# Moving the units that keep layer two's divided sums: out of layer one's output steps and some of layer two's token steps, into layer one's last token steps and its late mixing

## The chip, the cores and the metric

The kernel runs on one core of a Trainium2 chip. The metric is device microseconds of one execution; lower is better. A core has TensorE (PE: matmuls; its weight loads are listed apart as PEld), VectorE (DVE), ScalarE (ACT), GpSimd (POOL) and SyncE (SP). Each engine runs its own instructions in the order in which the program issues them, and waits on semaphores for what others make. SP does no arithmetic here: it issues DMA transfers, in order, and each issue can wait for the work that makes its data or frees its buffer.

## The reference, cut to what matters

Two layers, each a linear-attention block and a gated MLP whose gate mixes tokens (S = 2048 tokens, D = 512, FH = 896):

```python
x = x + _A_ref(_layernorm(x), A_wqkv, A_wo)                      # attention block
x = x + _B_ref(_layernorm(x), B_w_in, B_w_sp, B_b_sp, B_w_out)   # gated MLP
# ... the same two once more, with the same weights

def _B_ref(x, w_in, w_sp, b_sp, w_out):
    z = _gelu(x @ w_in)
    z1, z2 = z[..., :Fh], _layernorm(z[..., Fh:])
    g = einsum("ts,bsf->btf", w_sp, z2) + b_sp[None, :, None]    # mixing: 2048 x 2048 by 2048 x 896
    return (z1 * g) @ w_out
```

All is fp32. The kernel gets fp32's precision from three passes of the faster fp32r type: each operand is split into a high part (a copy on ScalarE) and a low part (the operand minus the high part, a subtraction on VectorE), and a product is high x high + high x low + low x high.

## The kernel before, in words

Each layer goes through four stages: `P1` (keys, queries, and the sum over tokens), `P2` (the token steps: attention output, norm, and the two halves of the MLP's input projection), the mixing (first part of `P4.run`), and the output steps (second part of `P4.run`: gate times `w_out`, added to x). Around 16 tiles of 128 tokens, `P2.run` makes 18 pipelined steps `s`; at step `s` it turns and splits the normalised input of tile `s-2` (`d_high`, `d_low`), projects tile `s-3` (`e`, the matmuls 448 wide), and takes up to two pieces of the other half (`f`).

The mixing doesn't do all eight block products of a 2 x 2 blocking but seven, on sums of blocks (P4, P2, P1, P6, P7, P5, P3, each of eight steps `g`; 56 in layer one). A step of P3 has 18 matmuls, one of P4, P2, P1 or P5 has 24. In step `g`, `prepare(g + 2, g + 3)` splits the weight operand of step `g+2` and the token operand of step `g+3`, then come the matmuls of step `g`, the load for step `g+4`, a gate product on POOL, and in P3's steps a piece of `w_out` (`wpiece`: a load on SP, a high part on ScalarE, a low part on VectorE). At the end of a product its banks are added up on VectorE (`evac`).

In layer two the product P2 is itself divided once more into seven smaller ones (the steps "N"). Four of these need sums of blocks of `w_sp`. The class `Inner` makes them ahead of time, already split, and keeps them in DRAM (`n1` to `n4`): 16 units, four for each of the block columns `k`. A call of `unit()` first finishes the unit before (low part on VectorE, then two stores on SP, one of the high and one of the low part), then adds or subtracts two blocks on VectorE and takes the high part on ScalarE, and may load a block. `begin(n)` loads the first blocks of `n` columns. The sums depend on the weights alone, so they can be made anywhere ahead of layer two's mixing.

The order on each engine is written out by hand: it is the order of these calls. Before, layer one's output steps 0 to 5 held one column (four units), and layer two's token steps 5 to 13 the other three (twelve units: one ahead of `d_low` in steps 6 to 12, one at the end of steps 7 to 11).

Of the kernel before, what the change touches and what calls it, by code (L numbers as in the profile page):

```python
# [53 lines left out]
def mixer_kernel(ctx: ExitStack, tc: tile.TileContext, x_in, wqkv, wo_d, win1_d, win2_d, wsp_d, bsp_d, wout_d,  # L54
# [45 lines left out]
    def high(h, src):  # L100
        nc.scalar.activation(h, src, AF.Copy)  # L101
# [503 lines left out]
    class P2:  # L605
# [309 lines left out]
        def run(self, sums):  # L915
            w1 = self.win1
            for s in range(1, NT + 3):
                self.loadx(s + 1)
                self.qturn.load(s + 1)
                if s in self.qturn.by_pe:  # L920
                    self.c(s - 1)
                    self.b_high(s)
                    self.c2(s - 1)
                    self.b_low(s)
                    self.c_stats(s - 1)
                    if s >= 2:
                        self.d_high(s - 2)
                        self.d_low(s - 2)
                    self.p1.late()
                    self.c3(s - 1)  # L930
                    self.a2(s + 2)
                    self.p1.late_phi()
                    self.a(s + 3)
                elif s - 2 in self.xturn.by_pe:
                    self.b_high(s)
                    self.c(s - 1)
                    self.c2(s - 1)
                    self.c_stats(s - 1)
                    self.a2_den(s + 2)
                    self.b_low(s)  # L940
                    self.a2_mul(s + 2)
                    self.d_high(s - 2)
                    self.d_low(s - 2)
                    self.c3(s - 1)
                    self.a(s + 3)
                else:
                    if s < NT:
                        self.b_high(s)
                    self.a2_den(s + 2)
                    if s < NT:  # L950
                        self.b_low(s)
                    if s <= NT:
                        self.c(s - 1)
                        self.c2(s - 1)
                        self.c_stats(s - 1)
                    if s == NT:
                        quads.put(*self.W2)
                        pages.put(self.zbc)
                    self.a2_mul(s + 2)
                    if s <= NT:  # L960
                        self.c3(s - 1)
                    self.a(s + 3)
                    if s <= NT + 1:
                        self.d_high(s - 2)
                        if self.seven and 6 <= s < 14:
                            inner.unit()
                        self.d_low(s - 2)
                if s >= 15:
                    self.block_sums()
                if 4 <= s <= 6:  # L970
                    self.e3(s - 4)
                if 5 <= s <= 7:
                    self.e4(s - 5)
                if s > 6:
                    self.e4(s - 4)
                self.xturn.load(s - 1)
                if s >= 3:
                    self.e(s - 3)
                    self.e2(s - 3)
                if s >= 6:  # L980
                    self.e3(s - 3)
                self.f()
                self.f()
                if self.seven:
                    self.side(s)
                    if s == 5:
                        inner.begin(3)
                    elif 7 <= s < 12:
                        inner.unit()
                self.fq.extend(self.fnext)  # L990
                self.fnext = []
                w1.piece(True)
                w1.fetch()
                if s == 7:
                    sums.fetch()
                if s > 7:
                    sums.tick()
                if s >= NT + 1 and not self.seven:
                    self.p4.fetch(s - NT - 1)
            self.e4(NT - 1)  # L1000
            self.win2.free()
# [49 lines left out]
    class Inner:  # L1051
# [31 lines left out]
        def unit(self):  # L1083

            self.finish()
            if not self.todo:
                return
            k, u = self.todo.popleft()
            if u == 0:
                self.S1 = t = self.raw.pop("22")  # L1090
                nc.vector.tensor_add(t, self.raw["21"], t)
            elif u == 1:
                t = self.raw.pop("21")
                nc.vector.tensor_sub(t, self.raw["11"], t)
            elif u == 2:
                self.S2 = t = self.raw.pop("11")
                nc.vector.tensor_sub(t, self.S1, t)
                pages.put(self.S1)
            else:
                t = self.raw.pop("12")  # L1100
                nc.vector.tensor_sub(t, t, self.S2)
                pages.put(self.S2)
            h = pages.get(PAGE, F32R)
            high(h, t)
            self.open = (1, 3, 2, 4)[u], k, h, t, u % 2 == 0
            if self.left:
                self.fetch()
                self.left -= 1

        def begin(self, n):  # L1110

            self.fetch()
            self.fetch()
            self.left = 4 * n - 2


    class P4:
# [336 lines left out]
        def run(self, nxt):  # L1454
            p2 = self.p2
            if p2.seven:
                p2.tail(self)
            else:
                self.prepare(0, 0)
                self.fetch(2)  # L1460
                while p2.f():
                    pass
                p2.win1.free()
                self.prepare(1, 1)
                self.fetch(3)
                self.prepare(None, 2)
            self.gb = [bigs.get([P, NF, 512]) for _ in range(NCHK)]
            n = len(self.steps)
            for g in range(n):
                p, k = self.steps[g]  # L1470
                self.prepare(g + 2, g + 3)
                if self.outs:
                    p2.gelu_out(*self.outs.popleft())
                self.mm(g)
                self.fetch(g + 4)
                if g in (1, 4, 7) or 8 <= g < 28:
                    self.sums.tick()
                if g == 3:
                    self.loadb()
                if self.nested and 4 <= g < 8:  # L1480
                    self.token_sums(g - 4)
                self.gates()
                if p == "P3":
                    if k < NF:
                        self.wpiece(k)
                    if k == 6:
                        self.loadx(0)
                        self.loadx(1)
                    if k == 7:
                        self.zsplit(0)  # L1490
                if p != "N" and k == HT - 1:
                    self.evac(p)
            pages.put(*self.bs)
            self.zsplit(1)
            make = Make() if nxt is not None else None
            for i in range(NT):
                self.loadx(i + 2)
                self.gates()
                if i == NT - 1 and nxt is not None:
                    nxt.T(1)  # L1500
                self.o(i)
                self.zsplit(i + 2)
                if make is not None:
                    if i == 0:
                        inner.begin(1)
                    elif i < 6:
                        inner.unit() if i < 5 else inner.finish()
                    make.step(i)
                if nxt is not None:
                    self.join(i, nxt)  # L1510
# [20 lines left out]
    inner = Inner()  # L1531
# [44 lines left out]
```

## Time and profile before

| | |
|---|---|
| median of 3 runs | 1385.32 us (1385.21 to 1387.07) |
| the profiled execution | 1387.32 us, its span 1385.6 us |
| granted TensorE clock | 1.0 throughout |

The stages of the profiled execution, in microseconds from the span's start:

| stage | from, to | PE busy | DVE busy | ACT busy | POOL busy |
|---|---|---|---|---|---|
| layer one, P1 | 0 to 138 | 135.4 | 99.3 | 89.0 | 49.2 |
| layer one, token steps | 138 to 331.4 | 193.4 | 134.8 | 84.8 | 88.7 |
| layer one, mixing | 331.4 to 622.3 | 290.9 | 191.7 | 105.4 | 113.0 |
| layer one, output steps | 622.3 to 699 | 76.4 | 53.6 | 24.3 | 10.1 |
| layer two, P1 | 699 to 828 | 129.0 | 91.2 | 82.3 | 44.9 |
| layer two, token steps | 828 to 1014.6 | 186.0 | 147.7 | 90.2 | 76.4 |
| layer two, mixing | 1014.6 to 1305.4 | 290.2 | 194.8 | 117.6 | 55.8 |
| layer two, output steps | 1305.4 to 1385.6 | 76.4 | 29.8 | 10.5 | 6.5 |

How the rows below are read. A row of the order of time has the start and the length in microseconds, the engine, the line of the kernel, the operation, the tile written and the tiles read, their shape, how many instructions are merged in it, and in brackets how long the engine had been idle before it and who ended that. "SPq" is an issue of a DMA; its length includes what it waited inside a merged group. A row of the waits has who waited for whom, the total in microseconds, how often, and the longest. In a row of the page's busy times x is the number of instructions. TensorE's matmuls overlap: a 512-wide one is listed with 0.39 us, though the next one starts 0.23 us later, so short slips between starts aren't counted as idle time.

### The profile page before, as it was taken

The numbers are of one execution on the slowest core, as the hardware profiler recorded it, in microseconds if no ns is written. First come the engines' busy times: TensorE is split into PE (matmuls) and PEld (weight loads), VectorE is DVE, ScalarE is ACT, GpSimd is POOL, SyncE is SP. The second block draws the span as 40 slices with busy tenths as digits, with TensorE's granted clock in tenths as the row PEclk, the third lists the DMA queues.
The fourth block names the chain that finished last, engine by engine and source line by source line (L and its number), as shares of the span: only waits on it lengthen the run. The fifth ranks groups of instructions, "written<-read, shape, count | busy, mean of one in ns | idle before, by whom it ended". The sixth has DMA issues, their size and how long they took to land. (4 is left out here: it accounts for less than half of the span.)

```text
span 1385.6 us, 17844 instructions
## 1 busy us (share of the span) xinstructions
PE 1377.7 (99%) x6209; PEld 1152.4 (83%) x6209; DVE 942.8 (68%) x1383; ACT 604.0 (44%) x944; POOL 444.6 (32%) x521
## 2 busy tenths in 40 slices
PE   9999999999999999999999999999999999999998
PEld 7888888888888888888888888888888888888887
DVE  6776887753756586677667768878668565775642
ACT  6674544334442234242357655534454432342410
POOL 3343454543135541431123335543130101133310
PEclk9999999999999999999999999999999999999999
DMA  5541366866678974357945414677465744544442
GB/s 174 170 131 61 116 188 228 254 211 211 221 235 293 292 234 134 134 205 250 349 130 150 132 54 146 229 251 259 142 205 171 263 159 131 173 131 158 167 145 91
DMA packets 158523, 255.54 MB, mean 184 GB/s; under 512 B 13408, under 2 KB 57312, under 8 KB 157408
## 3 DMA queue, kind: packets, MB, share of 16 engines
q1 hardware_dynamic: 153680, 239.59, 53.3%
q0 software_dynamic: 2880, 11.54, 2.6%
q10 hardware_dynamic: 1872, 3.28, 0.6%
q8 instruction: 48, 0.79, 0.2%
q14 instruction: 43, 0.35, 0.1%
HBM read 173.87 MB, written 80.48 MB: 184 GB/s over the span
## 5 line engine op out<-in xcount | busy, mean ns | idle before, releaser
L1345 PE MATMUL bank<-qd,pg 128*128 128x512 f32 x736 | 286.4, 389 | 0.2 <-DVE pg L890 0.2
L1347 PE MATMUL bank<-qd,pg 128*128 128x512 f32 x736 | 286.3, 389 | 0.0
L1346 PE MATMUL bank<-qd,pg 128*128 128x512 f32 x736 | 286.3, 389 | 0.0
L1211 DVE TENSOR_TENSOR qd<-qd,qd 128x1024 fp32r<-128x1024 f32 x110 | 154.7, 1406 | 123.2 <-ACT qd L1201 122.8
L1201 ACT ACTIVATE qd<-qd 128x1024 fp32r<-128x1024 f32 x110 | 116.5, 1059 | 232.7 <-DMA qd<-s 104.5
L1345 PEld LDWEIGHTS bank<-qd,pg 128*128 128x128 f32 x736 | 138.1, 188 | 29.3 <-DVE pg L890 0.6
L1346 PEld LDWEIGHTS bank<-qd,pg 128*128 128x128 f32 x736 | 138.1, 188 | 28.7
L1347 PEld LDWEIGHTS bank<-qd,pg 128*128 128x128 f32 x736 | 138.1, 188 | 28.7
L1367 POOL TENSOR_TENSOR bg<-bg,pg 128x512 f32<-128x512 f32 x56 | 81.9, 1466 | 238.0 <-DMA pg<-z 160.5
L117 PE MATMUL bank<-qd,pg 128*128 128x512 f32 x380 | 148.4, 390 | 0.0
L230 POOL TENSOR_SCALAR rs<-mv 128x1 f32<-128x1 f32 x95 | 40.8, 429 | 320.8 <-DVE mv L228 319.6
L1028 POOL TENSOR_TENSOR pg<-pg,pg 128x512 f32<-128x512 f32 x64 | 91.5, 1429 | 90.2 <-DMA pg<-in_wsp_dram 86.4
L241 ACT ACTIVATE pg<-pg,nb,rs 128x512 f32<-128x512 f32 x63 | 51.1, 811 | 148.1 <-POOL nb L235 137.4
L115 PE MATMUL bank<-qd,pg 128*128 128x512 f32 x284 | 110.7, 390 | 0.0
L116 PE MATMUL bank<-qd,pg 128*128 128x512 f32 x284 | 110.6, 389 | 0.0
L101 ACT ACTIVATE pg<-pg 128x512 fp32r<-128x512 f32 (+1 forms) x111 | 68.1, 617 | 95.5 <-DVE pg L292 39.5
L115 PE MATMUL bank<-bg,qd 128*128 128x448 f32 x256 | 94.3, 369 | 0.5 <-ACT qd L101 0.4
L117 PE MATMUL bank<-bg,qd 128*128 128x448 f32 x256 | 93.8, 366 | 0.2
L116 PE MATMUL bank<-bg,qd 128*128 128x448 f32 x256 | 93.6, 366 | 0.0
L292 DVE STREAM_TRANSPOSE pg<-pg 128x512 f32<-128x512 f32 x79 | 85.4, 1081 | 7.5 <-DMA pg<-xt 2.3
L104 DVE TENSOR_TENSOR pg<-pg,pg 128x512 fp32r<-128x512 f32 (+1 forms) x109 | 78.4, 723 | 15.7 <-ACT pg L101 13.7
L117 PE MATMUL bank<-wo,qd 128*128 128x512 f32 x224 | 87.2, 390 | 0.3 <-DVE qd L104 0.3
(186 smaller groups left out, 2845.2 us busy)
## 6 DMA issues: line engine op xcount, KB each, us to landing
qd<-s SPq DMA_DIRECT2D x64, 512.0 KB, 3.4
qd<-in_wsp_dram SPq DMA_DIRECT2D x46, 512.0 KB, 4.7
pg<-in_wsp_dram SPq DMA_DIRECT2D x80, 256.0 KB, 4.7
s<-pg SPq DMA_DIRECT2D x64, 256.0 KB, 4.6
pg<-x SPq DMA_DIRECT2D x64, 256.0 KB, 3.7
pg<-z SPq DMA_DIRECT2D x56, 256.0 KB, 3.9
x<-pg SPq DMA_DIRECT2D x48, 256.0 KB, 3.3
z<-pg SPq DMA_DIRECT2D x44, 256.0 KB, 2.7
```

The source lines that it names most:

```text
L104: nc.vector.tensor_sub(l, src, h.bitcast(F32))
L115: nc.tensor.matmul(out, ah, bh, start=start, stop=False)
L116: nc.tensor.matmul(out, ah, bl, start=False, stop=False)
L117: nc.tensor.matmul(out, al, bh, start=False, stop=stop)
L292: nc.vector.transpose(y.rearrange("p c (t m) -> p m c t", m=4), r.rearrange("p (m c j) -> p m c j", m=4, c=4))
L1028: nc.gpsimd.tensor_tensor(t, a, b, op=OP.add)
L1201: nc.scalar.activation(wh, r, AF.Copy)
L1211: nc.vector.tensor_sub(wl, r, wh.bitcast(F32))
L1345: m(out, h[:, o], w[:, 0, j, :], start=start, stop=False, skip_group_check=True)
L1346: m(out, h[:, o], w[:, 1, j, :], start=False, stop=False, skip_group_check=True)
L1347: m(out, l[:, o], w[:, 0, j, :], start=False, stop=stop, skip_group_check=True)
L1367: nc.gpsimd.tensor_tensor(u, u, z1, op=OP.mult)
```

## The change

One column of units (k = 0) moves from layer one's output steps to its token steps 14 to 18: `begin(1)` at the end of step 14, and calls of `unit` ahead of `d_low` in steps 15, 16 and 17 and at the end of steps 16 and 18 (the fifth call only finishes the fourth unit). The next column (k = 1) moves from layer two's token steps to layer one's mixing: `begin(1)` in step 43, `unit` in steps 45, 47, 49, 51 and 53, that is in the last three odd steps of the product P5 and in P3's steps 1, 3 and 5; the call stands after the gate product and ahead of `wpiece`. The other two columns stay in layer two's token steps: `begin(2)` at the end of step 6, `unit` ahead of `d_low` in steps 7 to 13 and at the end of steps 10 and 11. A counter `due` bounds the units that a `begin` allows. No arithmetic is added or taken away, and no matmul is touched.

```diff
@@ P2.run
                         self.d_high(s - 2)
-                        if self.seven and 6 <= s < 14:
+                        if (7 <= s < 14) if self.seven else (15 <= s < 18):
                             inner.unit()
                         self.d_low(s - 2)
...
                     self.side(s)
-                    if s == 5:
-                        inner.begin(3)
-                    elif 7 <= s < 12:
+                    if s == 6:
+                        inner.begin(2)
+                    elif s in (10, 11):
                         inner.unit()
+                elif s == 14:
+                    inner.begin(1)
+                elif s in (16, 18):
+                    inner.unit()
@@ Inner.unit
             self.finish()
-            if not self.todo:
+            if not self.due:
                 return
+            self.due -= 1
@@ Inner.begin
-            self.left = 4 * n - 2
+            self.due, self.left = 4 * n, 4 * n - 2
@@ P4.run
                 self.gates()
+                if not self.nested and 43 <= g < 54 and g % 2:
+                    inner.unit() if g > 43 else inner.begin(1)
                 if p == "P3":
...
                 if make is not None:
-                    if i == 0:
-                        inner.begin(1)
-                    elif i < 6:
-                        inner.unit() if i < 5 else inner.finish()
                     make.step(i)
```

## The prediction

> **What bounds the kernel now.** I read the page's head and its busy times first, then the waits of TensorE, then the order of starts on each engine around the places that the change touches.
>
> ```profile
> span 1385.6 us, 17844 instructions
> PE 1377.7 (99%) x6209; PEld 1152.4 (83%) x6209; DVE 942.8 (68%) x1383; ACT 604.0 (44%) x944; POOL 444.6 (32%) x521
> PEclk9999999999999999999999999999999999999999
> ```
>
> TensorE is busy for 1377.7 of 1385.6 us at the full granted clock. The change touches no matmul, so the time moves only by gaps between matmuls: those it closes and those it opens. The waits of TensorE (who waited for whom: us in total, times, longest) are few:
>
> ```profile
> PE bank L441 <- DVE pg L436: 2.4, 1, 2.4
> PE bank L115 <- ACT qd L101: 0.4, 1, 0.4
> PE bank L828 <- DMA pg<-win_sums: 0.4, 1, 0.4
> PE bank L117 <- DVE qd L104: 0.3, 1, 0.3
> PE bank L1345 <- DVE pg L890: 0.2, 1, 0.2
> ```
>
> The 2.4 us are the program's start. The other rows make 1.3 us, and there is more in starts that slip without a recorded wait, because a matmul's modelled end overlaps the next one's start. So there are only a few microseconds to win, and no limit to what can be lost.
>
> **Part 1: layer two's token steps, twelve units become eight.** A unit costs VectorE one addition and, one call later, the low part of its split. These are the second and third row below; the first and the last two are the low part of the normalised input (the second half of `d_low`) at the ends of steps 8, 10 and 13.
>
> ```profile
> 907.38 0.69 DVE L104 TENSOR_TENSOR qd<-pg,qd 128x512 fp32r<-128x512 f32 x1 [1.46 <-ACT qd L101]
> 938.04 0.64 DVE L104 TENSOR_TENSOR pg<-pg,pg 128x512 fp32r<-128x512 f32 x1
> 938.60 0.69 DVE L1091 TENSOR_TENSOR pg<-pg,pg 128x512 f32<-128x512 f32 x1
> 934.72 0.69 DVE L104 TENSOR_TENSOR qd<-pg,qd 128x512 fp32r<-128x512 f32 x1 [1.46 <-ACT qd L101]
> 971.66 0.69 DVE L104 TENSOR_TENSOR qd<-pg,qd 128x512 fp32r<-128x512 f32 x1 [1.54 <-ACT qd L101]
> ```
>
> TensorE reads that tile at the start of the next step's wide projection. Of its rows the first two follow one another at the start in step 9, the third is the start in step 11, and the last two pairs are places where a start slips:
>
> ```profile
> 911.76 0.36 PE L115 MATMUL bank<-bg,qd 128*128 128x448 f32 x1
> 911.96 0.37 PE L116 MATMUL bank<-bg,qd 128*128 128x448 f32 x1
> 935.15 0.36 PE L115 MATMUL bank<-bg,qd 128*128 128x448 f32 x1
> 971.99 0.37 PE L116 MATMUL bank<-bg,qd 128*128 128x448 f32 x1
> 972.41 0.47 PE L117 MATMUL bank<-bg,qd 128*128 128x448 f32 x1
> 999.41 0.39 PE L830 MATMUL bank<-qd,bg 128*128 128x512 f32 x1
> 1000.21 0.47 PE L115 MATMUL bank<-bg,qd 128*128 128x448 f32 x1 [0.41 <-ACT qd L101]
> ```
>
> The third matmul needs the low part, 0.4 us after the first. The lead is 911.76 + 0.4 - 908.07 = 4.1 us after step 8, but 935.15 + 0.4 - 935.41 = 0.1 us after step 10: with two units a step VectorE's round takes 934.72 - 907.38 = 27.3 us for two steps, TensorE's 23.4. At step 14 it is late: 971.99 to 972.41 is 0.42 where a 448-wide matmul takes 0.20, and 999.41 to 1000.21 is 0.80 where a 512-wide one takes 0.23. From 971 to 1001 I count eleven such slips, the two quoted among them, together 2.0 us. The same point in layer one, which has no units, has a lead of 318.77 + 0.4 - 313.84 = 5.3 us:
>
> ```profile
> 313.15 0.69 DVE L104 TENSOR_TENSOR qd<-pg,qd 128x512 fp32r<-128x512 f32 x1 [1.82 <-ACT qd L101]
> 318.77 0.36 PE L115 MATMUL bank<-bg,qd 128*128 128x448 f32 x1
> ```
>
> The change leaves one unit in each of steps 7 to 9, and steps 10 to 13 as they were. That saves three times 1.3 us ahead of step 10, so the lead there becomes about 4 to 5 us, and the slips of 2.0 us go. The later waits for `win_sums` (0.4) and for L890 (0.2) lie behind the same late chain; half of them and of their slips, 0.6 us, I count as gone. Part 1: **-2.6 us** (between -2.0 and -3.1).
>
> **Part 2: layer one's output steps lose four units.** There is one slip, the L117 wait in the list of waits:
>
> ```profile
> 655.87 0.39 PE L116 MATMUL bank<-wo,qd 128*128 128x512 f32 x1
> 656.51 0.50 PE L117 MATMUL bank<-wo,qd 128*128 128x512 f32 x1 [0.26 <-DVE qd L104]
> ```
>
> The starts are 0.64 apart where 0.23 is due, and the next one slips by 0.1. VectorE has 4 x (0.64 + 0.69) = 5.3 us less to do ahead of it. **-0.5 us**.
>
> **Part 3: layer one's token steps 15 to 18 get four units.** By the pair above the lead there is 5.3 us. Two units between two low parts delay it by 2.7 us on VectorE and, by two high parts on ScalarE, about 1.2 us; they overlap. On SP the eight stores stand ahead of the load of a turned tile, which waits for its own store's landing anyway. Cost 0; the lead is the cover, and if it were gone, up to 1 us.
>
> **Part 4: layer one's late mixing gets four units.** VectorE and ScalarE have room here. The danger is SP's queue. `finish` puts two stores on SP, and the second waits for VectorE's low part; everything behind it on SP waits too. In the output steps of before this is seen: SP's waits from 620 to 660 us, then SP in order of time, where the two stores hold the loads for 3.4 us.
>
> ```profile
> SPq L1079 <- DVE pg L104: 4.8, 3, 2.6
> 637.93 3.42 SPq L1079 DMA_DIRECT2D n<-pg  x2
> 641.44 0.38 SPq L97 DMA_DIRECT2D pg<-in_wsp_dram  x1
> ```
>
> There nothing urgent was behind it. In the last eight mixing steps (product P3, 4.08 us each: 18 matmuls at 0.227) the load of an output-weight piece is behind it in the same step, and ScalarE splits that piece ahead of the mixing operand of three steps on. The rows of before:
>
> ```profile
> 594.80 0.42 SPq L97 DMA_DIRECT2D pg<-in_wout_dram  x1
> 602.96 0.42 SPq L97 DMA_DIRECT2D pg<-in_wout_dram  x1
> 598.68 0.63 ACT L101 ACTIVATE wo<-pg 128x512 fp32r<-128x512 f32 x1 [2.20 <-DMA pg<-in_wout_dram]
> 599.22 1.05 ACT L1201 ACTIVATE qd<-qd 128x1024 fp32r<-128x1024 f32 x1
> 597.25 0.55 DVE L1217 TENSOR_TENSOR pg<-z_z,pg 128x384 fp32r<-128x384 f32 x1
> 599.35 0.69 DVE L104 TENSOR_TENSOR wo<-pg,wo 128x512 fp32r<-128x512 f32 x1 [1.55 <-ACT wo L101]
> 612.44 1.78 ACT L101 ACTIVATE qd<-bg 128x896 fp32r<-128x896 f32 x2
> 600.30 1.23 DVE L1211 TENSOR_TENSOR qd<-qd,qd 128x1024 fp32r<-128x1024 f32 x1 [0.26 <-ACT qd L1201]
> 606.00 0.39 PE L1345 MATMUL bank<-qd,pg 128*128 128x512 f32 x1
> 614.16 0.39 PE L1345 MATMUL bank<-qd,pg 128*128 128x512 f32 x1
> 622.32 0.39 PE L115 MATMUL bank<-wo,qd 128*128 128x512 f32 x1
> ```
>
> From the load's issue to the operand's low part: 600.30 + 1.23 - 594.80 = 6.7 us, 3.9 of them the transfer. Now step by step, numbering mixing steps from 0:
> - Step 49: the low part of `finish` follows the row at 597.25, so it ends at 598.4. The store goes then, and the piece is loaded at 598.95 instead of 594.80. Operand 52 is ready at 605.7; it is read from 606.0 (its low part from 606.2). Just covered.
> - Step 51: piece 2 (loaded at 600.3) and operand 53 are split after that, and `finish` ends at 609.2 on VectorE. Piece 3 is loaded at 609.7 instead of 602.96, so operand 54 is ready at 609.7 + 6.7 = 616.4. It is wanted at 614.4: TensorE stands **2.0 us**.
> - Step 53: piece 4 and operand 55 (1.05 on ScalarE, then 1.23 on VectorE) put `finish` at 619.3; piece 5 goes at 619.8 and piece 6 at 620.8, and the high part of the first output tile (half of the 1.78 us row) is behind them on ScalarE: 620.8 + 3.9 + 0.6 + 0.9 = 626.2, its low part a microsecond later. Output step 0 could begin at 622.3 + 2.0 = 624.3: another **2.5 us**, and **0.3** in the next output step, whose split waits behind six evacuations. Sum 4.8 us.
>
> One thing makes this larger. POOL's gate products share something with VectorE; while four of them run (second row), a low part of 0.55 us takes 1.65:
>
> ```profile
> 611.26 1.65 DVE L1217 TENSOR_TENSOR pg<-z_z,pg 128x384 fp32r<-128x384 f32 x1
> 608.64 7.12 POOL L1367 TENSOR_TENSOR bg<-bg,pg 128x512 f32<-128x512 f32 x4 [1.08 <-DMA pg<-z]
> ```
>
> In the late order the products fall onto these low parts. With 1.1 us for each of the two in steps 50 and 51 and again two further on, the same count gives 9 us. The Trainium skill ("SBUF — State Buffer", section "Who interferes with whom") has the rule: a VectorE instruction with two SBUF inputs and a GpSimd one that reads SBUF exclude each other for the whole instruction. The 1.65 us row agrees; by that rule alone the sum of this part would be the 9 us, without it the 4.8. How many products meet a low part is a matter of phase, so I take **+7 us** and keep 4.8 and 9 as ends.
>
> **Sum.** -2.6 - 0.5 + 0 + 7 = +3.9 us on the profiled execution, which took 1387.3 (its span and 1.7 around it): 1391.2. That execution stands 2.0 above the median of 1385.3; against the median it is **1389.2 us**.
>
> **Rivals.**
> - *B, faster: the mixing covers its units.* If piece 3 is on its way by 607.7 (614.4 - 6.7), 2.0 us sooner than I reckon, step 54 does not wait, and what follows is early too. The stores would then cost SP only their issue. For it: the 3.4 us block of before opened no gap of TensorE there but the one of 0.5. Against it: `finish` stands behind the low parts of its own step, and those behind the previous piece. Time: -2.5 to -3.6, 1381.7 to 1382.8. In the Trainium skill, "DMA: Bandwidth & Descriptors", section "Issuing engines are not separate DMA queues", the issuing engine's time is called usually small relative to the transfer; by that the stores would cost nothing here, and the 3.4 us row speaks against taking it so.
> - *C: layer two's lead doesn't come back*, since steps 10 to 12 still carry five units. Then -0.5 + 7: 1391.8. Against it: each of the three steps ahead of them loses 1.3 us on VectorE, and the lead after step 8 is 4.1 us even with two units a step.
> - *D: nothing shows*, the gaps that close and those that open being equal within 1 us, or the moved units changing no gap: 1385.
>
> **How the numbers follow.** My case has 0.68: 1386.5 (4.8 - 3.6) to 1391.8 (9 - 2.5); of it 0.55 is slower by over 0.2% (2.8 us, about what a measurement of this kernel can tell from none), 0.13 within. B has 0.17: 0.09 faster, 0.08 within. C has 0.10, slower. D has 0.05, within. Together: faster 0.09, within 0.26, slower 0.65. The range runs from B's 1382.5 to 1392.8, past C.
>
> **What would show it.** In layer one's last mixing steps SP's stores of the sums stand for microseconds before the loads of the output-weight pieces, TensorE waits at step 54 and at the first output step for low parts on VectorE, and the slips of 971 to 1001 us are gone from layer two. No gap from 295 to 350 us. I am wrong if the waits of TensorE name neither of the first two, or if the slips in layer two remain.

## The result and the profile after

The changed kernel takes 1391.53 us in the median (1391.31 to 1393.02, six runs), the kernel before 1385.86 (1385.21 to 1387.07, six runs): a ratio of 1.0042, with a 95% interval from 1.0029 to 1.0055. It is slower by 0.4%, by more than the 0.2% that a measurement of this kernel can tell. The profiled execution took 1391.97 us.

The page of the changed kernel begins so:

```profile
span 1390.3 us, 17858 instructions
PE 1378.1 (99%) x6209; PEld 1154.5 (83%) x6209; DVE 942.1 (68%) x1383; ACT 604.4 (43%) x944; POOL 443.4 (32%) x521
```

The span is 4.7 us longer. The counts on the engines are the same, and VectorE and ScalarE are as busy as before: the same work stands in other places. Lines have moved by four or five: the unit's stores are L1083 (L1079 before), the mixing's matmuls L1350 to L1352 (L1345 to L1347 before).

TensorE's waits in the changed kernel (who waited for whom: us in total, times, longest):

```profile
PE bank L441 <- DVE pg L436: 2.4, 1, 2.4
PE bank L1350 <- ACT qd L1206: 2.3, 1, 2.3
PE bank L115 <- ACT qd L101: 1.7, 1, 1.7
PE bank L1351 <- DVE qd L1216: 1.5, 1, 1.5
PE bank L117 <- DVE qd L104: 0.4, 1, 0.4
```

Apart from the program's start, all of it is new and lies in one place: the mixing's step 54 waits for its weight operand's high part (L1206) and then its low part (L1216), and the first output step waits for both parts of its tile (L101, L104). The waits of before for `win_sums`, for L890 and in layer two's token steps are gone.

SP's waits from 580 to 625 us name the cause, and SP's queue in order of time shows it:

```profile
SPq L1083 <- DVE pg L104: 19.4, 3, 9.6
```

```profile
594.78 3.94 SPq L1083 DMA_DIRECT2D n<-pg  x2
598.82 0.37 SPq L97 DMA_DIRECT2D pg<-in_wout_dram  x1
...
602.90 7.40 SPq L1083 DMA_DIRECT2D n<-pg  x2
610.35 0.42 SPq L97 DMA_DIRECT2D pg<-in_wout_dram  x1
...
612.32 10.36 SPq L1083 DMA_DIRECT2D n<-pg  x2
622.78 0.38 SPq L97 DMA_DIRECT2D pg<-in_wout_dram  x1
```

Three times a pair of stores holds the queue, for 3.9, 7.4 and 10.4 us, and each time the load of an output-weight piece stands right behind. Before, two of these pieces went at 594.80 and 602.96. The prediction had them at 598.95, 609.7 and 619.8; they went at 598.82, 610.35 and 622.78.

TensorE's starts at the three places where it stands, in order of time:

```profile
613.84 0.39 PE L1352 MATMUL bank<-qd,pg 128*128 128x512 f32 x1
616.50 0.50 PE L1350 MATMUL bank<-qd,pg 128*128 128x512 f32 x1 [2.28 <-ACT qd L1206]
618.50 0.50 PE L1351 MATMUL bank<-qd,pg 128*128 128x512 f32 x1 [1.49 <-DVE qd L1216]
...
627.96 0.39 PE L1352 MATMUL bank<-qd,pg 128*128 128x512 f32 x1
630.08 0.50 PE L115 MATMUL bank<-wo,qd 128*128 128x512 f32 x1 [1.74 <-ACT qd L101]
...
631.21 0.50 PE L117 MATMUL bank<-wo,qd 128*128 128x512 f32 x1 [0.40 <-DVE qd L104]
```

Starts are 0.23 us apart where nothing waits. The first two gaps are 2.66 and 2.00, so step 54 costs 2.44 + 1.77 = 4.2 us. The output step costs 2.12 - 0.23 = 1.9, and 0.8 over its next starts: 2.7 us.

After the first stand something else follows. The stretch from 618.90 to 622.31 us (PE, PEld, DVE, ACT and POOL busy with their numbers of instructions, granted clock, DMA):

```profile
618.90:622.31 3.41, 3.41 (x10) 2.65 (x9) 3.41 (x4) 0.00 (x0) 0.68 (x1) 0.50 0.03 5
```

The granted clock is 0.50 for 3.41 us. In it the starts are 0.43 apart instead of 0.23, which makes them 1.7 us late. So the late starts of the late mixing and what follows it sum to 4.2 + 1.7 + 2.7 = 8.6 us. Layer two's slips between 960 and 1045 us, 3.2 us when I sum all starts that were late before, are all gone, and so is the slip of the output steps (0.4 and 0.1, together 0.5): 8.6 - 3.2 - 0.5 = 4.9, against the spans' 4.7.

The 1.7 us of the half clock are a part of this sum, but by the profile they didn't make the kernel longer. The chain of work that ended last, followed back from the first output step, runs through loads, ScalarE, VectorE and SP's stores, and between 600 and 631 us no row of it is TensorE's. Its end:

```profile
623.75 4.78 DMA pg<-in_wout_dram
629.10 0.94 ACT qd L101
630.06 1.10 DVE qd L104
631.21 0.50 PE bank L117
```

At the full clock TensorE would have come to the first output step 1.7 us sooner and, as far as this chain shows, would have stood there 1.7 us longer.

### The profile page after: what moved, and what is told of

It reads as the page before. It is cut to its first block, busy times and chain, and to the rows that moved or that the text cites. A ratio compares the mean times of both kernels' runs of the same rounds, so it can differ in the third digit from the quotient of the medians.

```text
span 1390.3 us, 17858 instructions
## 1 busy us (share of the span) xinstructions
PE 1378.1 (99%) x6209; PEld 1154.5 (83%) x6209; DVE 942.1 (68%) x1383; ACT 604.4 (43%) x944; POOL 443.4 (32%) x521
## 4 chain that ended last, share of the span: by engine, by line
PE 97%; DMA 1%; DVE 1%; issue 0%; ACT 0%; SPq 0%; POOL 0%; DVEq 0%; ACTq 0%; POOLq 0%
PE bank L117 19%; PE bank L116 19%; PE bank L115 19%; PE bank L1352 11%; PE bank L1350 11%; PE bank L1351 11%; PE bank L1295 1%; PE bank L1292 1%; PE bank L1294 1%; PE bank L829 1%; PE bank L828 1%; PE bank L830 1%; DMA pg<-in_wout_dram 1%; PE bank L253 1%; PE bank L441 0%
## 5 line engine op out<-in xcount | busy, mean ns | idle before, releaser
L1350 PE MATMUL bank<-qd,pg 128*128 128x512 f32 x736 | 287.2, 390 | 2.3 <-ACT qd L1206 2.3
L1352 PE MATMUL bank<-qd,pg 128*128 128x512 f32 x736 | 287.0, 390 | 0.0
L1216 DVE TENSOR_TENSOR qd<-qd,qd 128x1024 fp32r<-128x1024 f32 x110 | 152.4, 1386 | 117.8 <-ACT qd L1206 117.3
L1206 ACT ACTIVATE qd<-qd 128x1024 fp32r<-128x1024 f32 x110 | 116.5, 1059 | 221.4 <-DMA qd<-s 94.2
L1350 PEld LDWEIGHTS bank<-qd,pg 128*128 128x128 f32 x736 | 138.5, 188 | 31.3 <-ACT qd L1206 2.7
L1352 PEld LDWEIGHTS bank<-qd,pg 128*128 128x128 f32 x736 | 138.5, 188 | 28.7
L101 ACT ACTIVATE pg<-pg 128x512 fp32r<-128x512 f32 (+1 forms) x111 | 68.3, 617 | 98.7 <-DVE pg L292 40.6
L115 PE MATMUL bank<-wo,qd 128*128 128x512 f32 x224 | 87.2, 390 | 1.7 <-ACT qd L101 1.7
L117 PE MATMUL bank<-wo,qd 128*128 128x512 f32 x224 | 87.3, 390 | 0.4 <-DVE qd L104 0.4
```

The costliest lines, as they stand in the source:

```text
L115: nc.tensor.matmul(out, ah, bh, start=start, stop=False)
L117: nc.tensor.matmul(out, al, bh, start=False, stop=stop)
L1206: nc.scalar.activation(wh, r, AF.Copy)
L1216: nc.vector.tensor_sub(wl, r, wh.bitcast(F32))
L1350: m(out, h[:, o], w[:, 0, j, :], start=start, stop=False, skip_group_check=True)
L1352: m(out, l[:, o], w[:, 0, j, :], start=False, stop=stop, skip_group_check=True)
```

## The experiments

Two theories were to be told apart for the 8.6 us: SP's in-order queue, which holds a load behind a waiting store; or the units' own work on VectorE and ScalarE and its meeting with POOL. For layer two: fewer units, or some other consequence.

**The stores one call later.** In layer one's mixing the two stores of a unit go at the next call of `unit`, when their low part is long made:

```diff
-        def unit(self):
+        def unit(self, hold=False):
-            self.finish()
+            self.store()          # the stores held at the call before
+            self.finish(hold)     # hold: low part now, stores at the next call
...
@@ P4.run
-                    inner.unit() if g > 43 else inner.begin(1)
+                    inner.unit(True) if g > 43 else inner.begin(1)
+                if not self.nested and g == 55:
+                    inner.store()
```

> The changed kernel, but in layer one's mixing the two stores of a unit are issued one call later than its low part is made, so SP never waits for VectorE there. All work, its steps and its transfers stay. Theory (SP's in-order queue holds the output-weight loads back): the waits of TensorE at mixing step 54 and at the first output step go, with the half-clock stretch behind them; what is left are the gains in layer two (3.2 us) and in the output steps (0.6 us): 1382 to 1383 us against 1385.9 before. Rival (the units' own work on VectorE and ScalarE, and the gate products that meet it, make the operands late): TensorE still stands several us, 1388 to 1391 us.

Measured: 1383.95 us against 1386.49 before, ratio 0.9980 (0.9972 to 0.9989). TensorE's waits behind the start:

```profile
PE bank L1361 <- DVE qd L1226: 0.8, 1, 0.8
```

L441 and L472 wait in the first 12 us, at the program's start, and aren't listed here. All steps of VectorE and ScalarE are there, and 0.8 us of waiting is left at step 54; its late starts sum to 1.3 us of the 8.6. The queue is the cause of nearly all of it; the work alone is not. The gain, 2.5 us, falls short of the 2.9 to 3.9 expected, since that wait didn't go whole. SP's waits from 590 to 622 us say where the rest may come from:

```profile
SPq L97 <- DVE wo L104: 3.9, 3, 2.2
SPq L97 <- DMA n<-pg: 3.8, 2, 2.0
```

The loads now wait for their pages: a unit that keeps its two pages for two steps longer leaves fewer free ones, and a load has to wait until a page's last reader, a store among them, is done. That these waits make the 0.8 us was not tried apart.

**The pieces loaded earlier.** The other side of the same pair: the stores stay and SP waits for them as before, but the output-weight pieces are loaded three steps sooner, in steps 45 to 51.

```diff
                 self.gates()
+                self.wfetch(g - (n - HT) + (0 if self.nested else 3))
...
+        def wfetch(self, f):
+            if 0 <= f < NF:
+                self.wraw[f] = load(wout_d[f * P:(f + 1) * P, :])
...
         def wpiece(self, f):
-            r = load(wout_d[f * P:(f + 1) * P, :])
+            r = self.wraw.pop(f)
```

> The changed kernel with the output-weight pieces of layer one loaded three mixing steps earlier (steps 45 to 51 instead of 48 to 54), each ahead of the unit of its step. The units and their stores stay where the changed kernel has them, and SP still waits there. Theory (what hurts is that the piece's load stands behind the waiting store): TensorE's wait at step 54 falls to 1.3 us or less, what was left with the stores issued later; 1382.5 to 1384.5 us. Rival (what hurts is the hold-up of the other loads, of mixing operands and of gate tiles, or of VectorE): 1388 to 1391 us.

Measured: 1383.31 us against 1386.05, ratio 0.9980 (0.9972 to 0.9989). TensorE has no wait behind the start. SP's waits for low parts from 580 to 625 us:

```profile
SPq L1083 <- DVE pg L104: 6.6, 2, 3.5
```

SP still waits 6.6 us for low parts, and TensorE waits nowhere but at the start. Here the blocked queue cost nothing, with the pieces no longer behind the stores. The waits also feed themselves: with the pieces in time the stores wait 6.6 us, in the changed kernel 19.4, where each late piece makes the next low part late.

**The units earlier in the mixing.** Steps 31 to 41 instead of 43 to 53, where no pieces are loaded:

```diff
-                if not self.nested and 43 <= g < 54 and g % 2:
-                    inner.unit() if g > 43 else inner.begin(1)
+                if not self.nested and 31 <= g < 42 and g % 2:
+                    inner.unit() if g > 31 else inner.begin(1)
```

> The changed kernel with the mixing's four units in steps 31 to 41 (products P7 and early P5) instead of 43 to 53. Theory: no output-weight load is behind the stores there, and VectorE runs up to two steps ahead of TensorE, so SP hardly waits: 1382 to 1383 us. Rival (any unit in the mixing costs, since a store that waits also holds the operands' loads): waits of TensorE in steps 35 to 45, 1386 to 1391 us.

Measured: 1383.37 us against 1386.49, ratio 0.9977 (0.9967 to 0.9986). TensorE's one wait is that of the start, and from 520 to 580 us SP waits 1.3 us for the low parts:

```profile
PE bank L441 <- DVE pg L436: 2.4, 1, 2.4
```

```profile
SPq L1083 <- DVE pg L104: 1.3, 1, 1.3
```

So units in the mixing are not dear in themselves. The expected reason, that VectorE runs ahead there and has made the low part before SP comes to its store, agrees with the short wait of SP, but wasn't tried apart from the missing pieces.

**Part 4 undone.** The second column stands in the output steps, as the first did before; the token steps of both layers are the changed kernel's.

```diff
-                if not self.nested and 43 <= g < 54 and g % 2:
-                    inner.unit() if g > 43 else inner.begin(1)
...
                 if make is not None:
+                    if i == 0:
+                        inner.begin(1)
+                    elif i < 6:
+                        inner.unit()
                     make.step(i)
```

> The changed kernel with part 4 alone undone: the second column's four units stand in layer one's output steps, as the first column's did before. Theory: no gap in the late mixing, the slip of 0.6 us in the output steps is back, layer two keeps its gain of 3.2 us: 1382.5 to 1383.5 us. Rival (layer two's gain only came from the long stand ahead of it, not from its fewer units): 1385.5 to 1386 us, with slips in layer two's token steps 14 to 17.

Measured: 1383.52 us against 1386.49, ratio 0.9978 (0.9969 to 0.9987). TensorE has no wait behind the start. The stand in the mixing is gone and layer two keeps its gain. One expectation failed: the slip of the output steps is not back, though four units stand there again. So the units as such don't make that half microsecond; what does isn't shown.

**Part 4 alone.** The kernel before, with the four units of the output steps put into mixing steps 43 to 53; layer two keeps twelve.

```diff
                 self.gates()
+                if not self.nested and 43 <= g < 54 and g % 2:
+                    (inner.begin(1) if g == 43 else inner.unit() if g < 53 else inner.finish())
...
-                    if i == 0:
-                        inner.begin(1)
-                    elif i < 6:
-                        inner.unit() if i < 5 else inner.finish()
```

> The kernel before with one thing changed: the four units of layer one's output steps stand in mixing steps 43 to 53 as in the changed kernel; layer two keeps its twelve units. Theory: the same 8.6 us as in the changed kernel open between mixing step 52 and the second output step (about 1.7 of them the half clock), the 0.6 us slip of the output steps goes, layer two's 3.2 us stay: 1393 to 1394.5 us. Rival (the stand comes from the combination with the token steps' units, or layer two's gain is a consequence of it): 1389 to 1391 us, with layer two's slips gone.

Measured: 1395.23 us (1393.36 to 1397.38) against 1386.49, ratio 1.0062 (1.0049 to 1.0075). TensorE's waits, without the start and those under 0.4 us:

```profile
PE bank L115 <- ACT qd L101: 2.7, 2, 2.3
...
PE bank L1345 <- ACT qd L1201: 2.0, 1, 2.0
PE bank L1346 <- DVE qd L1211: 0.8, 1, 0.8
PE bank L828 <- DMA pg<-win_sums: 0.4, 1, 0.4
PE bank L117 <- DVE qd L104: 0.4, 1, 0.4
```

The late starts from 600 to 640 us sum to 8.1 us, half clock included; layer two's slips (3.5 us) and its wait for `win_sums` are there again. The kernel takes 8.7 us more than before, a little over the 7.1 to 8.6 expected, and its runs scatter over 4 us. Within that the two parts add up, and neither needs the other.

**Without the gate products.** To size the meeting with POOL: the changed kernel without POOL's products in layer one's mixing steps 50 to 55, their loads kept. Six gate tiles are then not multiplied by the gate.

```diff
-                self.gates()
+                self.gates(not self.nested and g >= 50)
...
-                nc.gpsimd.tensor_tensor(u, u, z1, op=OP.mult)
+                if not skip:
+                    nc.gpsimd.tensor_tensor(u, u, z1, op=OP.mult)
```

> The changed kernel without POOL's gate products in layer one's mixing steps 50 to 55; the loads of their tiles stay. (Six gate tiles are then not multiplied by the gate.) Theory (products and low parts exclude each other and lengthen the chain): TensorE stands 2.0 us at step 54 and 2.5 to 2.8 us at the first output steps, the sum without products, and the stand is too short for the half clock: 3.8 us less than the changed kernel, about 1387.7 us. Rival (the products cost nothing, the chain of loads alone makes the 8.6 us): as the changed kernel, 1391.5 us.

Measured: 1388.07 us against 1386.05, ratio 1.0017 (1.0008 to 1.0027): 0.25% or 3.5 us better than the changed kernel's 1.0042. TensorE's waits without the start:

```profile
PE bank L115 <- ACT qd L101: 1.6, 1, 1.6
PE bank L1351 <- DVE qd L1216: 0.8, 1, 0.8
PE bank L1350 <- ACT qd L1206: 0.7, 1, 0.7
PE bank L117 <- DVE qd L104: 0.4, 1, 0.4
```

The late starts sum to 4.6 us here (2.0 and 2.6), without a half clock. The same low parts on VectorE and the products on POOL in the changed kernel, and then without products:

```profile
607.71 1.64 DVE L1222 TENSOR_TENSOR pg<-z_z,pg 128x384 fp32r<-128x384 f32 x1
616.48 1.96 DVE L1216 TENSOR_TENSOR qd<-qd,qd 128x1024 fp32r<-128x1024 f32 x1 [0.25 <-ACT qd L1206]
606.97 1.97 POOL L1372 TENSOR_TENSOR bg<-bg,pg 128x512 f32<-128x512 f32 x1 [0.94 <-DMA pg<-z]
615.67 3.92 POOL L1372 TENSOR_TENSOR bg<-bg,pg 128x512 f32<-128x512 f32 x2 [6.73 <-DMA pg<-z]
```

```profile
607.77 0.55 DVE L1222 TENSOR_TENSOR pg<-z_z,pg 128x384 fp32r<-128x384 f32 x1
614.90 1.22 DVE L1216 TENSOR_TENSOR qd<-qd,qd 128x1024 fp32r<-128x1024 f32 x1 [0.26 <-ACT qd L1206]
```

1.64 against 0.55 and 1.96 against 1.22: VectorE's instruction is lengthened when a product runs on POOL. By the Trainium skill, "SBUF — State Buffer", section "Who interferes with whom", a VectorE instruction with two SBUF inputs and a GpSimd one that reads SBUF exclude each other. The trace agrees: the low part that begins at 607.71 ends 0.4 us after the product's end at 608.94, and the product too is lengthened, to 1.97 us from the 1.29 of the one at 593.81, which meets no low part.

The chain to the first output step shows where the 4.0 us between 8.6 and 4.6 come from. Three low parts on it are longer with products: those at 607.71 and 616.48 by 1.1 and 0.7 us, and the one at 618.36 (1.63 against 0.55) by 1.1, together 2.9. The other 1.1 us are two loads of pieces that landed 0.6 and 0.6 us later after their issue; whether the products have a part in that isn't shown.

**The token steps alone.** The kernel before, with the four units of the output steps put into layer one's token steps 15 to 18; layer two keeps twelve.

```diff
-                        if self.seven and 6 <= s < 14:
+                        if (6 <= s < 14) if self.seven else (15 <= s < 18):
                             inner.unit()
...
+                elif s == 14:
+                    inner.begin(1)
+                elif s == 16:
+                    inner.unit()
+                elif s == 18:
+                    inner.finish()
...
-                    if i == 0:
-                        inner.begin(1)
-                    elif i < 6:
-                        inner.unit() if i < 5 else inner.finish()
```

> The kernel before with one thing changed: the four units of layer one's output steps stand in its token steps 15 to 18. Nothing in the mixing; layer two keeps its twelve units. Theory: no gap from 295 to 350 us, the 0.6 us slip of the output steps goes, layer two's 3.2 us of slips stay: 0.5 us less than before, 1385.5 to 1386 us. Rival (the token steps' lead doesn't cover four units): gaps there and 1387 us or more. Second rival (layer two's gain comes from elsewhere than its own units): 1382.5 to 1383.5 us.

Measured: 1385.86 us against 1386.05, ratio 1.0000 (0.9991 to 1.0008): no difference that can be told. TensorE's waits behind the start:

```profile
PE bank L115 <- ACT qd L101: 0.4, 1, 0.4
PE bank L1351 <- DVE pg L890: 0.2, 1, 0.2
```

No gap from 295 to 350 us and none in the output steps; layer two's late starts are 2.8 us here. Between this kernel and the one with part 4 undone the main difference is a column in layer two, and they stand 0.22% apart (1.0000 and 0.9978), 3.0 us.

## Why the prediction was right

The forecast was 1389.2 us, 3.9 more than before, with a chance of 0.65 for slower by over 0.2%; measured were 1391.5 and 5.7 more. Its case and its mechanism hold: stores that wait on SP, pieces behind them, and TensorE standing at step 54 and at the first output step. No rival came true. The 1391.5 us are nearly rival C's 1391.8, but by chance: C's reason, that layer two's lead doesn't come back, failed. The range's lower end, 1382.5, left out most of rival B's own 1381.7 to 1382.8, which didn't matter here.

- **Part 1, layer two.** Predicted -2.6, with a lead of 4 to 5 us from step 10 on. Low parts on VectorE after steps 10 and 13, and the starts on TensorE that need them:

```profile
937.48 0.69 DVE L104 TENSOR_TENSOR qd<-pg,qd 128x512 fp32r<-128x512 f32 x1 [1.46 <-ACT qd L101]
974.76 0.69 DVE L104 TENSOR_TENSOR qd<-pg,qd 128x512 fp32r<-128x512 f32 x1 [1.53 <-ACT qd L101]
```

```profile
943.19 0.36 PE L115 MATMUL bank<-bg,qd 128*128 128x448 f32 x1
979.63 0.36 PE L115 MATMUL bank<-bg,qd 128*128 128x448 f32 x1
```

  The lead is 943.19 + 0.4 - 938.17 = 5.4 us (0.1 before) and 979.63 + 0.4 - 975.45 = 4.6 us. All slips went, those of the tail too, of which I had counted half: -3.2 us. The kernel with part 4 undone keeps this gain and the one with the token steps alone lacks it: it comes from the four units taken out of layer two.
- **Part 2, the output steps.** Predicted -0.5; the slip of 0.5 did go. But it stays away with four units there as well, so the reason given, that VectorE has less to do, is not shown.
- **Part 3, layer one's token steps.** Predicted 0, covered by a lead of 5.3 us. No gap opened, here or with these units alone. The lead at the last tile:

```profile
322.68 0.68 DVE L104 TENSOR_TENSOR qd<-pg,qd 128x512 fp32r<-128x512 f32 x1
```

```profile
326.29 0.36 PE L115 MATMUL bank<-bg,qd 128*128 128x448 f32 x1
```

  It is 326.29 + 0.4 - 323.36 = 3.3 us: the units used part of it.
- **Part 4, the late mixing.** Predicted +7, between 4.8 without meetings with POOL and 9 with four of them; measured +8.6. The count without products is confirmed by the kernel without them (4.6 us against 4.8). The mis-sized step is the number of products that meet a low part: I took the middle, and where four meetings make the 9, three lay on the chain, for 2.9 us, with 1.1 more from slower loads. That the stands alone, 4.2 + 2.7 = 6.9, come out at the 7 is luck. The half clock, which the prediction didn't have, makes up the other 1.7 us of the late starts, but TensorE wasn't on the chain there, so without it the second stand would by the profile have been 1.7 us longer.
- **The sum.** By the late starts it should have said -3.2 - 0.5 + 8.6 = +4.9 instead of +3.9; the spans say +4.7. The rest of the distance to the 5.7 us between the medians is in the choice of executions: the profiled execution of before stands 1.5 above the median of its six runs, that of after 0.4 above its own.

Freed of the late pieces, the change is a gain: 1383.3 to 1383.5 us with the pieces loaded earlier, the units earlier in the mixing, or the second column in the output steps, 0.2% less than before. These three differ by less than can be told.

## What to carry to other kernels

Here TensorE was 99% busy, and the same small work on the other engines cost nothing that can be told in layer one's token steps, in its earlier mixing and in its output steps, and 8.6 us of late starts where it touched an order. For each DMA that is put on a queue, ask what it waits for and what is queued behind it, and how far ahead of need that is. A store that waits for a late low part, ahead of a load that the next low part needs, makes each round later than the one before; loading a few steps earlier, storing a call later, or another place for the work each removed it. Where an engine's lead shrinks to nothing over some rounds, as in layer two, taking a few small pieces of work out of the rounds ahead got all of it back.

## What was not expected of the hardware

TensorE's clock went to half after two waits that were short by themselves. In the changed kernel the gaps between starts are 2.66 and 2.00 us with a single matmul between them, and the clock is 0.50 from 618.90 for 3.41 us. In the kernel with part 4 alone they are 2.4 and 1.3 us, and there too (the same columns as above):

```profile
618.38:621.79 3.41, 3.41 (x10) 2.64 (x9) 3.41 (x3) 0.35 (x1) 1.83 (x2) 0.50 0.02 5
```

Without products the gaps at the same place are 1.1 and 1.3 us, and with the stores later there is one of 1.3 us: the clock stayed at full speed. It stayed there too after the changed kernel's stand at the first output step, with gaps of 2.1 and 0.8 us and two matmuls between them. The Trainium skill, "TensorE: Matmul & The Clock Gate", section "HAM oscillation — how this bites in real kernels", puts the limit at idle gaps over about 3.4 us, the length of the window in which activity is watched. The 3.41 us of half clock agree with that window. The gaps do not: none was over 2.7 us; two of them with a single matmul between, 3.7 and 4.7 us together, were enough.

What tells these cases apart is how long TensorE was busy within stretches of 3.41 us on a fixed grid. In both kernels the fall comes 610.99 us after the clock first reached its full speed (at 7.91 and at 7.39 us), which is 179 times 3.413. The last stretch before it in the changed kernel, the stretch over that kernel's first output step, and the last stretch before the fall with part 4 alone (TensorE's busy time, matmuls, granted clock, DMA):

```profile
615.49:618.90 3.41, 0.91 (x3) 1.00 0.30 115
629.14:632.55 3.41, 2.07 (x8) 1.00 0.48 182
```

```profile
614.97:618.38 3.41, 1.32 (x5) 1.00 0.60 225
```

So the clock fell after 0.91 and 1.32 us of work in 3.41, and not after 2.07. Laid over the traces of all nine kernels, the grid has five whole stretches with 1.35 us of work or less, three of them at a kernel's end, and each was followed by the half clock; after every stretch with 1.91 us or more the clock stayed. That is an inference from these nine traces. Where between 1.35 and 1.91 us the limit lies isn't shown, and no run moved the gaps against the grid.
